# Thresholded attention and a rational feed-forward on one core: each batch by halves of its queries, and the first batch's probabilities transposed by float32 products

## The chip, the cores and the metric

One core of one Trainium2 chip runs the whole program. The metric is the device time of one execution in microseconds (us); lower is better. Three runs of the kernel before took 1432.35, 1436.73 and 1437.20 us, median 1436.73.

## The reference

There are 8 batches of 8 heads, 576 queries and keys, 64 numbers a head; the feed-forward goes from 512 to 2048 and back to 512 over 4608 tokens. Everything is float32.

```python
scores = q @ k.T / 8                                  # per batch and head
thresh = scores.max(-1) - tau                         # tau = 0.02
scores = where(scores >= thresh, scores, -1e9)
attn = exp(scores - scores.max(-1)); attn /= attn.sum(-1) + 1e-9
x = (attn @ v)                                        # heads side by side: 4608 x 512
h = x @ w_in
P = a[0] + a[1]*h + a[2]*h**2 + a[3]*h**3
Q = 1 + abs(b[0])*abs(h) + abs(b[1])*h**2
out = (P / (Q + 1e-6)) @ w_out
```

## The kernel before

**Units.** Heads go in pairs, so there are 4 pairs a batch and 32 in all (`bp`, 0 to 31). A pair's 576 queries are five units `t`: four of 128 queries (`NT` = 4) and one of the last 64, in which both heads share the 128 rows. `units` (line 504) lists them pair after pair, all five of a pair together. `pos` (lines 505 to 510) gives each its place on a scale on which a full unit counts 1 and a short one 0.5; a batch is 18 long.

**One unit** (`unit_ops`, line 611). TensorE makes the scores in float32 from QQ and KK (`f_qk`, lines 657 and 668). VectorE takes the row maxima (`f_max`: line 679 for both heads at once, line 681 for one, which the first `SINGLE` units use). ScalarE applies the threshold as a very steep Prelu (`f_pre`, line 694) and the exponential with its row sums (`f_sum`, line 698), both into a buffer `e`. The reciprocal of the sum (lines 703 to 709) scales the probabilities, which are split into a float16 high half (`f_hi`, in the buffer `hi`, written by the helper `times`, lines 280 and 282) and a low half (`f_lo`, line 720, over `e`). Both halves are transposed by DMA from the SP queue (`f_tp`, line 730) into `pT`, which holds two units. When two units are there, TensorE multiplies them with V (`f_av`, line 745): five key blocks, three float16 products for each (high by high, low by high, high by low) and each head, the two heads in different halves of the output rows. The result is split into a high and a low half of x (`f_xh`, `f_xl`, lines 753 to 759).

**V.** `load_v_ops` (line 551) loads the V tile of a pair into one of five buffers in turn (`bp % NV`), each load after the attention product that last read the buffer. When the four tiles of a batch are there, their largest absolute value gives a scale (`scale_ops`), and each tile is split into float16 halves (`split_v_ops`, lines 589 and 592).

**Q and K.** `load_ops` (line 528) loads QQ and KK of a pair once, five DMAs, from the SP queue for the first 8 pairs (`EARLY_BP`) and from POOL's queue after that; there are two buffers of each.

**Weights.** w_in and w_out come as 16 pieces of 512 KB each from POOL's queue into tiles of the pool `t`, and are decoded to float32 by ScalarE and VectorE (`decode_ops`, line 401); w_in is then scaled and split into float16 halves (lines 477 to 489). They form four blocks of 4 + 4 pieces, one for each 512 of the hidden width. `WHEN` (line 32) says for each block at which place its first piece is due and by how much the next ones follow.

**Feed-forward.** x is gathered in chunks of 256 tokens: two for the full units of each batch, ("m", batch, half), with units 0 and 1 in half 0 and units 2 and 3 in half 1, and one for the short units of four batches, ("r", ...). `moe_ops` (line 822) is one step: four slices of 128 of the hidden width for one chunk, with 48 float16 products (line 852), the rational function on ScalarE and VectorE (lines 861 to 906) and 8 float32 products with w_out (line 913, two records each). A chunk takes four steps, so there are 18 chunks and 72 steps. `last_g1` ties the steps' first products into one fixed order (`todo`): batch 0's chunks in the order of `FIRST`, then every chunk of batch b in the course of batch b + 1, and the last batch's three in the order of `LAST` behind the attention. A chunk that is interrupted leaves a partial sum, which `f_o` (line 915) evicts.

**The order.** Nothing is written out by hand. Each operation (`op`) has one engine or a choice (`FLEX`, with an estimated duration on each), a key (its due place), what it waits for, and the buffers and PSUM banks that it takes and gives back (`Hold`; `POOLS` has the number of each). `Plan.order` (line 131) simulates the engines with these durations and delays and at each moment emits the operation that can start first, the one with the lower key where several can. Buffers of a pool are handed out in the order of `rank`. Where TensorE would stand idle in the first 400 us of the plan it puts in warming products that multiply an identity (`f_warm`, line 1041). On the chip every engine runs its own list in that order and waits on semaphores. Plain DMAs and the transposes of the SP queue go out in order, as do those of POOL's queue ("GD" in the plan).

Of the kernel before, what the change touches and what calls it, by code (L numbers as in the profile page):

```python
# [23 lines left out]
POOLS = {"e": 4, "hi": 3, "pT": 2, "st": 8, "sc": 2, "t": 11, "u": 3, "x": 4, "xr": 1}  # L24
# [16 lines left out]

EARLY_BP = 8

STEEP = 2.0 ** 100

UP = 2.0 ** -14
TPD = 1.3

AHEAD_RANK = 2.0
# [7 lines left out]
        "vl": {"DVE": 0.75}, "xh": {"ACT": 0.31, "DVE": 0.31}, "xhr": {"ACT": 0.18, "DVE": 0.12}, "A": {"ACT": 0.541, "DVE": 0.345}, "r": {"ACT": 0.74, "DVE": 0.345},  # L57
# [30 lines left out]
class Plan:  # L88
# [42 lines left out]
    def order(self):  # L131
# [20 lines left out]
        while left:  # L152
# [78 lines left out]
def masked_attention_rational_ffn(  # L231
# [28 lines left out]
    for name, n in [*POOLS.items(), ("q", NQ), ("k", NQ)]:  # L260
        plan.pool(name, n)
# [242 lines left out]
    units = [(bp, t) for bp in range(NBP) for t in range(NT + 1)]  # L504
# [8 lines left out]
    NV = 5  # L513
# [5 lines left out]
    sx = const.tile([P, B], F32, name="sx")  # L519
    for t in Vs:  # L520
        nc.gpsimd.memset(t[:, NT * P:], 0.0)
    kq = {}
    av_done = {}
# [4 lines left out]
    def load_ops(bp):  # L528
        bb, pr = divmod(bp, NP)
        p = pos[(bp, 0)]  # L530
        plan.rank = p - 3.0
        kh, qh = kq[bp] = Hold("k", 2 * NT + 1), Hold("q", 2 * NT + 1)
        first = bp == 0
        p0 = p - (4.6 if first else 4.0)
        queue, eng = (nc.sync, "DMA") if bp < EARLY_BP else (nc.gpsimd, "GD")

        def ldq():
            QQ = QQs[qh.slot]
            queue.dma_start(QQ[0:D, 0:S], qT[bb, pr, :, 0:S])
# [9 lines left out]
        k_done[bp] = [op(eng, 1.1, p0 + 0.1, ldk, (), [kh])]  # L549

    def load_v_ops(bp):
        bb, pr = divmod(bp, NP)
        plan.rank = pos[(bb * NP, 0)]
        t = Vs[bp % NV]
        queue, eng = (nc.sync, "DMA") if bp < EARLY_BP else (nc.gpsimd, "GD")

        def ld():
            queue.dma_start(
                t[:, 0:NT * P].rearrange("p (c d) -> p c d", c=NT),
                v[bb, 0:NT * P, pr * P:(pr + 1) * P].rearrange("(c p) d -> p c d", p=P))  # L560
# [5 lines left out]
        def mx():  # L566
            if bb not in vms:
# [6 lines left out]
        q = pos[(bp, 0)] - 17.0  # L574
        l = op(eng, 1.6, max(q, -2.0 + 0.1 * pr), ld, [av_done.get(bp - NV)])
        hv = [Hold("u", 1)]
        vm_ops.setdefault(bb, []).append(op(FLEX["vmax"], 0, max(q + 1.0, p - 1.0), mx, [l], hv, hv))
        if pr == NP - 1:
            isx_done[bb] = scale_ops(p, lambda: vms[bb], 14, isx[:, bb:bb + 1], sx[:, bb:bb + 1], vm_ops[bb], f"x{bb}")
            for i in range(NP):  # L580
                split_v_ops(bb * NP + i)

    def split_v_ops(bp):
        bb, pr = divmod(bp, NP)
        p = max(pos[(bp, 0)] - 2.0, pos[(bb * NP, 0)])
        t, th = Vs[bp % NV], VHs[bp % NV]

        def vh():
            times(th, t, sx[:, bb:bb + 1])

        def vl():
            nc.vector.scalar_tensor_tensor(t.bitcast(F16)[:, 0:VW], t, sx[:, bb:bb + 1], th, ALU.mult, ALU.subtract)
        o = op(FLEX["vh"], 0, p, vh, [isx_done[bb]])
        v_done[bp] = op(FLEX["vl"], 0, p + 0.1, vl, [o])
# [16 lines left out]
    def unit_ops(bp, t):  # L611
# [3 lines left out]
        single = bp * (NT + 1) + t < SINGLE  # L615
        heads = (0, 1) if full else (0,)
        kh, qh = kq[bp]
        VL, VH = Vs[bp % NV].bitcast(F16)[:, 0:VW], VHs[bp % NV]
# [3 lines left out]
        e_hold = Hold("e", 1)  # L622
# [108 lines left out]

        def f_av():
            pT = place(two["pT"])
            box["av"] = bank(bhs["av"])[:, 0:w2]
# [15 lines left out]
        def f_xh():  # L750
            x = x_tile(ck)[0][:, pr, xo:xo + w2]
            if plan.eng == "ACT":
# [4 lines left out]
        def f_xl():  # L757
            xh, xl = x_tile(ck)
            nc.vector.scalar_tensor_tensor(xl[:, pr, xo:xo + w2], box["av"], UP, xh[:, pr, xo:xo + w2],
# [31 lines left out]
        his, los = [], []  # L791
        for hh in heads:
            his.append(op(FLEX["hi"], 0, p + 0.5 + 0.02 * hh, lambda hh=hh: f_hi(hh), [rec] + his, [hi_hold] if hh == 0 else ()))
            los.append(op("DVE", 0.68, p + 0.55 + 0.02 * hh, lambda hh=hh: f_lo(hh), his + los, (), [st_hold]))
        if not full:
            his.append(op("DVE", 0.13, p + 0.55, lambda: f_twice("hi"), his))
            los.append(op("DVE", 0.13, p + 0.6, lambda: f_twice("lo"), los))
        tp = op("DMA", TPD if full else 0.6 * TPD, p + 0.6, lambda: f_tp("hi"), his + two["tp"], [two["pT"]] if t % 2 == 0 else (),
                [hi_hold])
        tp = op("DMA", TPD if full else 0.6 * TPD, p + 0.65, lambda: f_tp("lo"), los + [tp], (), [e_hold])  # L800
        two["tp"].append(tp)
# [3 lines left out]
        av = op("PE", 2.0 if full else 0.7, p + 1.2, f_av, two["tp"] + [v_done[bp]], [bh], [two["pT"]])  # L805
        av_done[bp] = av
# [5 lines left out]
        xh = op(FLEX["xh" if full else "xhr"], 0, p + 1.4, f_xh, [av] + ([x_done[ck][0]] if not first else []), first, [bh])  # L812
# [9 lines left out]
    def moe_ops(ck, f0, nb, p, begins, ends, soon):  # L822
# [4 lines left out]
        plan.rank = p = max(p, w_key(g, 2 * NC))  # L827
# [87 lines left out]
        def f_o(tt, old):  # L915
# [3 lines left out]
            else:  # L919
                o = place(obox[tt]["hold"])  # L920
                nc.scalar.activation(o, acc[tt], AF.Copy, scale=-1.0)
# [53 lines left out]
        if ends:  # L975
            prev = None
            obox = {}
            for tt in range(2):
                old = sums.get((ck, tt))
                obox[tt] = {}  # L980
                if old is None:
                    ho = obox[tt]["hold"] = Hold("u", 1)
                    o = op("ACT", 0.5, p + 0.2 * nb + 1.8, lambda tt=tt, old=old: f_o(tt, old), [last_g2[tt], prev], [ho], [ah[tt]])
# [4 lines left out]
                if f0 + nb == NF:  # L988
# [5 lines left out]
    load_ops(0)  # L994
    for i in range(NP):
        load_v_ops(i)
    for bp, t in units:
        unit_ops(bp, t)
        if t == NT and bp + 1 < NBP:
            load_ops(bp + 1)  # L1000
        if t == NT and bp + NP < NBP:
            load_v_ops(bp + NP)
    todo = []
    for bb in range(B):
# [5 lines left out]
        last = pos[(bb * NP + NP - 1, NT)]  # L1010
# [4 lines left out]
        steps = []  # L1015
        if bb % 4 == 0 and bb:
            steps += [(("r", bb // 4 - 1, 0), f) for f in range(0, NF, NC)]
        if bb:
            steps += [(("m", bb - 1, c), f) for c in range(2) for f in range(0, NF, NC)]
        p0 = pos[(bb * NP, 0)] + LEAD  # L1020
        step = NP * 4.5 / len(steps) if steps else 0
        if bb == 1:

            steps = [(("m", 0, c), f) for c, f0, f1 in FIRST for f in range(f0, f1, NC)]
            step -= LEAD0 / len(steps)
            p0 += LEAD0
        todo += [(ck, f, NC, p0 + i * step) for i, (ck, f) in enumerate(steps)]
# [56 lines left out]
```

## Time and profile before

| | |
|---|---|
| median of three runs | 1436.73 us |
| the profiled execution, its own time | 1437.0 us |
| its span, first to last instruction | 1435.2 us |
| TensorE (PE) busy | 1365.4 us, 95%, 9130 instructions |
| VectorE (DVE) busy | 1194.6 us, 83% |
| ScalarE (ACT) busy | 1164.4 us, 81% |
| GpSimd (POOL) busy | 165.4 us, 12% |
| mean granted TensorE clock | 0.976 |
| read from and written to HBM | 45.09 MB and 9.44 MB |
| transposes issued | 320, each 3.3 us from issue to landing in the median |

The page gives busy time of each engine, also in 40 equal slices (a digit is tenths of the slice), the granted clock, and the share of the 16 DMA engines in use. "PEld" are weight loads, which run beside products. Busy time by stretch can be asked for any span of time and for one line alone. The waits name the engine and line that waited, what ended the wait, and total, times and longest. A line such as 280, 282 or 287 is that of a helper and serves several operations.

### The profile page before, as it was taken

How to read it: one execution, taken by the hardware profiler on the slowest of the kernel's cores; microseconds unless marked ns; L12 is line 12 of the kernel's file. 1: busy time of each engine (PE TensorE's matmuls, PEld its weight loads, DVE VectorE, ACT ScalarE, POOL GpSimd, SP SyncE). 2: the span in 40 equal slices, each digit the busy share in tenths (PEclk: the TensorE clock that was granted, in tenths of full speed). 3: DMA queues.
4: the chain of work that ended last, by engine and by line, in shares of the span. 5: the costliest groups of instructions: out<-in, count | busy, mean ns of one | idle time of the engine just before them, and what ended most of it. 6: DMA issues, size and time to landing. Idle time of an engine off the chain costs nothing. (4 is left out here: it accounts for less than half of the span.)

```text
span 1435.2 us, 24320 instructions
## 1 busy us (share of the span) xinstructions
PE 1365.4 (95%) x9130; PEld 859.8 (60%) x9130; DVE 1194.6 (83%) x1782; ACT 1164.4 (81%) x2078; POOL 165.4 (12%) x310
## 2 busy tenths in 40 slices
PE   8489889999999999999999999999999999999998
PEld 6366666566565566646666656665665656575664
DVE  5488798989987979788888987898987988896665
ACT  6489999999898988889768777889888978874553
POOL 3100111111111010111010111102011100000000
PEclk8698999999999999999999999999999999999999
DMA  8986775555565454545343354536555464420000
GB/s 238 141 167 125 154 165 120 121 101 121 105 115 101 82 114 91 100 101 115 73 89 80 74 90 92 114 65 131 90 97 112 82 108 93 90 43 16 15 16 15
DMA packets 371749, 142.12 MB, mean 99 GB/s; under 512 B 353328, under 2 KB 358576, under 8 KB 371632
## 3 DMA queue, kind: packets, MB, share of 16 engines
q1 hardware_dynamic: 355248, 93.11, 37.6%
q0 software_dynamic: 16384, 47.46, 12.5%
q8 instruction: 72, 1.18, 0.3%
q14 instruction: 45, 0.37, 0.1%
HBM read 45.09 MB, written 9.44 MB: 38 GB/s over the span
## 5 line engine op out<-in xcount | busy, mean ns | idle before, releaser
L913 PE MATMUL banks<-wp,t 128*128 128x512 f32 x1152 | 527.2, 598 | 4.3 <-DVE t L906 3.3
L852 PEld LDWEIGHTS <-wi 128*128 128x128 f16 x3456 | 336.6, 99 | 88.7 <-issue 52.1
L852 PE MATMUL banks<-x,wi 128*128 128x256 f16 x3072 | 362.5, 273 | 3.9 <-ACT t L861 1.7
L913 PEld LDWEIGHTS banks<-wp,t 128*128 128x128 f32 x1152 | 206.5, 190 | 209.8 <-issue 200.9
L720 DVE SCALAR_TENSOR_TENSOR e<-e,st,hi 128x576 f16<-128x576 f32 x288 | 234.1, 813 | 14.8 <-ACT hi L280 10.8
L694 ACT ACTIVATE e<-banks,st,cf 128x576 f32<-128x576 f32 x288 | 231.5, 825 | 17.7 <-DVE st L688 12.7
L657 PE MATMUL banks<-KK,QQ 64*128 64x512 f32 (+3 forms) x784 | 224.4, 552 | 22.0 <-ACT e L694 18.2
L698 ACT ACTIVATE e<-e,cf 128x576 f32<-128x576 f32 x288 | 220.7, 772 | 0.4
L280 ACT ACTIVATE hi<-e,st 128x576 f16<-128x576 f32 x254 | 190.6, 769 | 24.3 <-DVE st L709 20.0
L745 PE MATMUL banks<-pT,VH 128*64 128x256 f16 (+1 forms) x1920 | 136.3, 254 | 29.6 <-DMA pT<-e 28.7
L861 ACT ACTIVATE t<-banks,hsc 128x512 f32<-128x512 f32 (+1 forms) x192 | 106.1, 574 | 71.0 <-PE banks L852 70.5
L657 PEld LDWEIGHTS banks<-KK,QQ 64*128 64x128 f32 (+1 forms) x784 | 91.3, 194 | 117.9 <-issue 50.5
L679 DVE TENSOR_REDUCE st<-banks 128x2 f32<-128x1152 f32 x108 | 145.7, 1349 | 16.4 <-PE banks L668 16.1
L745 PEld LDWEIGHTS <-VH 128*64 128x64 f16 x1920 | 87.0, 112 | 62.1 <-issue 48.2
L891 ACT ACTIVATE t<-t,cf 128x1024 f32<-128x1024 f32 (+1 forms) x73 | 82.8, 1134 | 39.7 <-DVE t L888 39.4
L745 PE MATMUL banks<-pT,V 128*64 128x256 f16 (+1 forms) x960 | 109.4, 252 | 0.0
L668 PEld LDWEIGHTS banks<-KK,QQ 128*128 128x128 f32 x432 | 56.3, 190 | 81.9 <-issue 81.9
L900 DVE SCALAR_TENSOR_TENSOR t<-t,t 128x1024 f32<-128x1024 f32 (+1 forms) x73 | 88.0, 1205 | 15.3 <-ACT t L894 14.8
L906 DVE SCALAR_TENSOR_TENSOR t<-t,cf,t 128x1024 f32<-128x1024 f32 (+1 forms) x73 | 92.5, 1267 | 0.8
L897 DVE SCALAR_TENSOR_TENSOR t<-t,cf,t 128x1024 f32<-128x1024 f32 (+1 forms) x73 | 92.3, 1265 | 0.2
L888 DVE TENSOR_TENSOR t<-t,t 128x1024 f32<-128x1024 f32 (+1 forms) x73 | 87.9, 1205 | 2.8 <-ACT t L873 2.6
L903 DVE SCALAR_TENSOR_TENSOR t<-t,t 128x1024 f32<-128x1024 f32 (+1 forms) x73 | 88.0, 1206 | 0.8
(93 smaller groups left out, 1422.6 us busy)
## 6 DMA issues: line engine op xcount, KB each, us to landing
t<-in_w_in_dram POOLq DMA_DIRECT2D x16, 512.0 KB, 5.7
t<-in_w_out_dram POOLq DMA_DIRECT2D x16, 512.0 KB, 5.7
out_dram<-u POOLq DMA_DIRECT2D x32, 256.0 KB, 2.7
KK<-in_kT_dram POOLq DMA_DIRECT2D x48, 144.0 KB, 4.3
V<-in_v_dram POOLq DMA_DIRECT2D x24, 256.0 KB, 4.1
QQ<-in_qT_dram POOLq DMA_DIRECT2D x24, 144.0 KB, 3.0
QQ<-in_qT_dram POOLq DMA_DIRECT2D x24, 128.0 KB, 3.6
pT<-hi SPq DMA_TRANSPOSE x160, 3.3
```

The source lines that it names most:

```text
L280: nc.scalar.activation(dst, src, AF.Identity, scale=factor)
L657: nc.tensor.matmul(dst, QQ[r, c0:c0 + P], KK[r, k0:k1], **kw)
L679: nc.vector.tensor_reduce(box["st"][:, 0:2], box["both"], AX.X, ALU.max, negate=True)
L694: nc.scalar.activation(ev(hh), box["s"][hh], AF.Prelu, scale=qscale, bias=box["st"][:, 2 + hh:3 + hh], alpha=STEEP)
L698: nc.scalar.activation(e, e, AF.Exp, bias=ntau, accum_out=box["st"][:, 4 + hh:5 + hh])
L720: nc.vector.scalar_tensor_tensor(box["lo"][:, c], ev(hh), box["st"][:, 6 + hh:7 + hh], box["hi"][:, c], ALU.mult, ALU.subtract)
L745: nc.tensor.matmul(dst, V[:, c * P + hh * D:c * P + (hh + 1) * D], rhs, start=c == 0 and n == 0, stop=c == NT and n == 2)
L852: nc.tensor.matmul(d, wi_tile(c, f0 + j, hl), x[:, c, :], start=c == 0 and n == 0, stop=c == NC - 1 and n == 2)
L861: nc.scalar.activation(box["h3"][:, 2 * k:2 * k + 2, sl], psv[:, :, sl], AF.Identity, scale=hsc[:, b2, g:g + 1])
L897: nc.vector.scalar_tensor_tensor(box["r"], box["r"], a1, box["h"], ALU.add, ALU.mult)
L906: nc.vector.scalar_tensor_tensor(box["r"], box["r"], a0, box["q"], ALU.add, ALU.mult)
L913: nc.tensor.matmul(acc[tt], box["r"][:, o:o + P], wo[f], start=begins and j == 0, stop=ends and j == nb - 1)
```

## The change

**Order.** A batch is now visited in seven visits: pairs 0, 1 and 2 with units 0 and 1 only, pair 3 with all five units, then pairs 2, 1 and 0 with units 2, 3 and 4. `load_ops` runs once a visit, so q and k of three pairs of each batch are loaded twice. The V buffers become a pool of five that each V tile takes and gives back after the last of its three attention products. `VISITED` = 8 makes all batches go this way.

**Transposes.** In the first batch (`is_plain`: pairs 0 to 3, units 0 to 3) the probabilities are not split and not transposed by DMA. VectorE writes the identity times the reciprocal sum of each row (`f_diag`), TensorE multiplies each 128 by 128 block of e with it (`f_tr`, ten float32 products in three banks), and three evictions bring the result to `pT` in float32 (`f_ev`). The attention product then is ten float32 products with the V tile as loaded (`f_avp`), and x is scaled by another factor. The first batch's short units go as before, and V is split when these need it.

**Feed-forward.** Chunk ("m", 0, 0) starts with its first two steps, then follow the four of ("m", 0, 1), then the other two. From there every step's key is at least `SPACING` = 1.9679 behind the one before (3.0642 in batch 0) and `LEAD` = 0.8676 behind the last unit of its chunk. The partial sums of the interrupted chunk share one tile of the pool `t`.

**Weights, pools, constants.** The weights' due places move from (-3.82, 14.74, 15.84, 25.03) to (-3.45, 5.0, 11.9, 15.21). `e` has 3 buffers for 4, `hi` 2 for 3, `u` 4 for 3, `xr` 2 for 1. The plan counts a DMA of the SP queue that starts before 120 us at twice its duration and 1 us more. Priorities between ScalarE and VectorE change.

```diff
-POOLS = {"e": 4, "hi": 3, "pT": 2, "st": 8, "sc": 2, "t": 11, "u": 3, "x": 4, "xr": 1}
+POOLS = {"e": 3, "hi": 2, "pT": 2, "st": 8, "sc": 2, "t": 11, "u": 4, "x": 4, "xr": 2}
...
-LEAD, LEAD0 = 2.88, 0.04
-ENDK, ENDS = 1.2, 1.3
+LEAD, SPACE0, SPACING = 0.8676, 3.0642, 1.9679
+ENDK, ENDS = 3.4139, 5.1328
-WHEN = [(-3.82, 1.63), (14.74, 0.95), (15.84, 1.27), (25.03, 1.06)]
-SINGLE = 25
-FIRST = [(0, 0, 12), (1, 0, 16), (0, 12, 16)]
+WHEN = [(-3.45, 1.43), (5.0, 0.76), (11.9, 0.29), (15.21, 0.9)]
+V0, V1 = -2.1791, 0.6179
+SINGLE = 22
+VISITED = 8
+FIRST = [(0, 0, 8), (1, 0, 16), (0, 8, 16)]
+NV = 5
+PLAIN = (0, 1, 2, 3)
-AHEAD_RANK = 2.0
+AHEAD_RANK = 2.54
...
-EARLY = {"ACT": 2.4, "DVE": 6}
-EARLY_END = 250
-PRICE = {"ACT": 1.0, "DVE": 2.0}
+EARLY = {"ACT": 2.3035, "DVE": 3.83}
+EARLY_END = 543.1302
+PRICE = {"ACT": 0.6687, "DVE": 1.9849}
+LOADS_END = 120.0
...
+            if e == "DMA" and t < LOADS_END:
+                o.dur = 2.0 * o.dur + 1.0
...
-    units = [(bp, t) for bp in range(NBP) for t in range(NT + 1)]
+    half, rest = list(range(NT // 2)), [NT]
+    other = list(range(NT // 2, NT))
+    visits = []
+    for bb in range(B):
+        v0 = bb * NP
+        if bb < VISITED:
+            visits += [(v0 + i, half) for i in range(NP - 1)] + [(v0 + NP - 1, half + other + rest)]
+            visits += [(v0 + i, other + rest) for i in range(NP - 2, -1, -1)]
+        else:
+            visits += [(v0 + i, half + other + rest) for i in range(NP)]
+    units = [(bp, t) for bp, ts in visits for t in ts]
...
-        e_hold = Hold("e", 1)
+        e_hold = Hold("e", (3 if full else 2) if is_plain(bp, t) else 1)
...
+        def f_diag(hh):
+            if hh == 0:
+                box["dg"] = place(dg_hold)
+            nc.vector.tensor_scalar(box["dg"][:, hh * P:(hh + 1) * P], ident, box["st"][:, 6 + hh:7 + hh], None, ALU.mult)
+        def f_tr(piece, hold):
+            e, d = box["e"], bank(hold)
+            if piece < 2:
+                for c in range(NT):
+                    k = piece * (S + REM) + c * P
+                    nc.tensor.matmul(d[:, c * P:(c + 1) * P], e[:, k:k + P], box["dg"][:, piece * P:(piece + 1) * P],
+                                     start=True, stop=True)
+            else:
...
+        def f_ev(piece, hold):
+            pT = flat(two)
+            c0, n = ((0, NT), (NT + 1, NT), (NT, 1))[piece]
+            copy(pT[:, c0:c0 + n, t % 2, :], bank(hold)[:, 0:n * P].rearrange("p (c k) -> p c k", c=n))
...
+        def f_avp():
+            pT, V = flat(two), Vs[vh_[bp].slot]
+            box["av"] = bank(bhs["av"])[:, 0:w2]
+            for c in range(NT + 1):
+                for hh in range(2):
...
+                    nc.tensor.matmul(dst, V[:, c * P + hh * D:c * P + (hh + 1) * D], rhs, start=c == 0, stop=c == NT)
...
+        if plain:
+            pieces = (0, 1, 2) if full else (0, 2)
+            dg_hold = Hold("u", len(pieces))
...
+            for piece in pieces:
+                hold = Hold("b", 1, B1)
+                tr = op("PE", 0.9 if piece < 2 else 0.3, p + 0.5, lambda x=piece, h=hold: f_tr(x, h), [dg], [hold],
+                        [e_hold, dg_hold])
...
-    load_ops(0)
-    for i in range(NP):
-        load_v_ops(i)
-    for bp, t in units:
-        unit_ops(bp, t)
-        if t == NT and bp + 1 < NBP:
-            load_ops(bp + 1)
-        if t == NT and bp + NP < NBP:
-            load_v_ops(bp + NP)
+    for bp in range(NBP):
+        load_v_ops(bp)
+    for bp, ts in visits:
+        load_ops(bp, ts)
+        for t in ts:
+            unit_ops(bp, t)
...
+    order = [(("m", 0, c), range(f0, f1, NC)) for c, f0, f1 in FIRST]
+    for bb in range(1, B - 1):
+        order += [(("m", bb, c), range(0, NF, NC)) for c in range(2)]
+        if bb % 4 == 3:
+            order.append((("r", bb // 4, 0), range(0, NF, NC)))
+    p = 0.0
+    for ck, fs in order:
...
+        ready = max(pos[x] for x in last) + LEAD
+        for f in fs:
+            p = max(p + (SPACE0 if bb == 0 else SPACING), ready)
+            todo.append((ck, f, NC, p))
```

More of the change, by code (lines that the diff above doesn't have):

```diff
@@ L259, in masked_attention_rational_ffn @@
     op = plan.op
-    for name, n in [*POOLS.items(), ("q", NQ), ("k", NQ)]:
+    for name, n in [*POOLS.items(), ("q", NQ), ("k", NQ), ("v", NV)]:
         plan.pool(name, n)
@@ L519, in masked_attention_rational_ffn @@
     sx = const.tile([P, B], F32, name="sx")
+    sxu = const.tile([P, 1], F32, name="sxu")
     for t in Vs:
         nc.gpsimd.memset(t[:, NT * P:], 0.0)
-    kq = {}
-    av_done = {}
+    kq, vh_, v_loaded, plain_av = {}, {}, {}, {}
     k_done, q_done, v_done, isx_done = {}, {}, {}, {}
@@ L526, in masked_attention_rational_ffn, with load_ops @@
     pairs = {}
-    def load_ops(bp):
+    def load_ops(bp, ts):
         bb, pr = divmod(bp, NP)
-        p = pos[(bp, 0)]
+        p = pos[(bp, ts[0])]
         plan.rank = p - 3.0
-        kh, qh = kq[bp] = Hold("k", 2 * NT + 1), Hold("q", 2 * NT + 1)
-        first = bp == 0
+        n = sum(2 if t < NT else 1 for t in ts)
+        kh, qh = kq[bp] = Hold("k", n), Hold("q", n)
+        first = p == 0
         p0 = p - (4.6 if first else 4.0)
@@ L549, in load_ops, with is_plain, v_low @@
         k_done[bp] = [op(eng, 1.1, p0 + 0.1, ldk, (), [kh])]
+    def is_plain(bp, t):
+        return bp < NP and t in PLAIN
+    v_ops = {}
+    def v_low(bp):
+        if bp not in v_done:
+            p, o, vl = v_ops[bp]
+            v_done[bp] = op(FLEX["vl"], 0, p + 0.1, vl, [o] + plain_av.get(bp, []))
+        return v_done[bp]
     def load_v_ops(bp):
@@ L614, in unit_ops @@
         full = t < NT
-        single = bp * (NT + 1) + t < SINGLE
+        single = units.index((bp, t)) < SINGLE
         heads = (0, 1) if full else (0,)
         kh, qh = kq[bp]
-        VL, VH = Vs[bp % NV].bitcast(F16)[:, 0:VW], VHs[bp % NV]
+        plain = is_plain(bp, t)
         nh = len(heads)
@@ L730, in f_tp, with flat @@
             nc.sync.dma_start_transpose(place(two["pT"])[:, t % 2, part == "lo", 0:nb, :], box[part][:, 0:nb * P])
+        def f_diag(hh):
[11 more added lines that the diff above has]
+                for hh in range(2):
+                    k, dg = (NT * P + hh * REM, hh) if full else (NT * P, 0)
+                    nc.tensor.matmul(d[hh * D:(hh + 1) * D, 0:P], e[:, k:k + REM], box["dg"][:, dg * P:(dg + 1) * P],
+                                     start=True, stop=True)
+        def f_ev(piece, hold):
+            pT = flat(two)
+            c0, n = ((0, NT), (NT + 1, NT), (NT, 1))[piece]
+            copy(pT[:, c0:c0 + n, t % 2, :], bank(hold)[:, 0:n * P].rearrange("p (c k) -> p c k", c=n))
+        def flat(two):
+            return place(two["pT"]).rearrange("p a b c d -> p (a b c d)").bitcast(F32).rearrange(
+                "p (c u k) -> p c u k", c=2 * NT + 1, u=2)
+        def f_avp():
+            pT, V = flat(two), Vs[vh_[bp].slot]
+            box["av"] = bank(bhs["av"])[:, 0:w2]
+            for c in range(NT + 1):
+                for hh in range(2):
+                    pp = slice(hh * D, (hh + 1) * D)
+                    dst = box["av"][pp, :]
+                    if full:
+                        rhs = pT[:, c if hh == 0 or c == NT else NT + 1 + c, :, :]
+                        dst = dst.rearrange("p (u k) -> p u k", u=2)
+                    else:
+                        rhs = pT[:, c, 0, hh * REM:(hh + 1) * REM]
+                    nc.tensor.matmul(dst, V[:, c * P + hh * D:c * P + (hh + 1) * D], rhs, start=c == 0, stop=c == NT)
         def f_av():
             pT = place(two["pT"])
+            VL, VH = Vs[vh_[bp].slot].bitcast(F16)[:, 0:VW], VHs[vh_[bp].slot]
             box["av"] = bank(bhs["av"])[:, 0:w2]
@@ L751, in f_xh @@
             x = x_tile(ck)[0][:, pr, xo:xo + w2]
-            if plan.eng == "ACT":
+            if plain:
+                times(x, box["av"], sxu)
+            elif plan.eng == "ACT":
                 nc.scalar.activation(x, box["av"], AF.Copy, scale=UP)
@@ L790, in unit_ops @@
         rec = op("DVE", 0.103, p + 0.4, f_rec2, [rec])
[L791 to L801, printed above, removed]
+        if plain:
+            pieces = (0, 1, 2) if full else (0, 2)
+            dg_hold = Hold("u", len(pieces))
+            dg = None
+            for hh in heads:
+                dg = op("DVE", 0.14, p + 0.45, lambda hh=hh: f_diag(hh), [rec, dg], [dg_hold] if hh == 0 else (), [st_hold])
+            for piece in pieces:
+                hold = Hold("b", 1, B1)
+                tr = op("PE", 0.9 if piece < 2 else 0.3, p + 0.5, lambda x=piece, h=hold: f_tr(x, h), [dg], [hold],
+                        [e_hold, dg_hold])
+                take = [two["pT"]] if not two["tp"] and t % 2 == 0 else ()
+                two["tp"].append(op(FLEX["ev" if piece < 2 else "ev1"], 0, p + 0.55, lambda x=piece, h=hold: f_ev(x, h),
+                                    [tr] + two["tp"][:1], take, [hold]))
+        else:
+            his, los = [], []
+            for hh in heads:
+                his.append(op(FLEX["hi"], 0, p + 0.5 + 0.02 * hh, lambda hh=hh: f_hi(hh), [rec] + his, [hi_hold] if hh == 0 else ()))
+                los.append(op("DVE", 0.68, p + 0.55 + 0.02 * hh, lambda hh=hh: f_lo(hh), his + los, (), [st_hold]))
+            if not full:
+                his.append(op("DVE", 0.13, p + 0.55, lambda: f_twice("hi"), his))
+                los.append(op("DVE", 0.13, p + 0.6, lambda: f_twice("lo"), los))
+            tp = op("DMA", TPD if full else 0.6 * TPD, p + 0.6, lambda: f_tp("hi"), his + two["tp"], [two["pT"]] if t % 2 == 0 else (),
+                    [hi_hold])
+            tp = op("DMA", TPD if full else 0.6 * TPD, p + 0.65, lambda: f_tp("lo"), los + [tp], (), [e_hold])
+            two["tp"].append(tp)
@@ L804, in unit_ops @@
         bh = bhs["av"] = Hold("b", 2, B1)
-        av = op("PE", 2.0 if full else 0.7, p + 1.2, f_av, two["tp"] + [v_done[bp]], [bh], [two["pT"]])
-        av_done[bp] = av
+        if plain:
+            av = op("PE", 2.6 if full else 0.7, p + 1.2, f_avp, two["tp"] + [v_loaded[bp]], [bh], [two["pT"], vh_[bp]])
+            plain_av.setdefault(bp, []).append(av)
+        else:
+            av = op("PE", 2.0 if full else 0.7, p + 1.2, f_av, two["tp"] + [v_low(bp)], [bh], [two["pT"], vh_[bp]])
         if ck not in xh_hold:
@@ L811, in unit_ops @@
             first = []
-        xh = op(FLEX["xh" if full else "xhr"], 0, p + 1.4, f_xh, [av] + ([x_done[ck][0]] if not first else []), first, [bh])
+        xh = op(FLEX["xh" if full else "xhr"], 0, p + 1.4, f_xh, [av, isx_done["up"]] + ([x_done[ck][0]] if not first else []), first, [bh])
         xl = op("DVE", 0.36 if full else 0.16, p + 1.5, f_xl, [xh], (), [bh])
@@ L826, in moe_ops @@
         g = f0 // NC
[L827 removed]
+        plan.rank = p = max(p, w_key(g, 2 * NC) - 1.0)
         name = f"{kind}{bb}_{half}_{f0}"
@@ L977, in moe_ops @@
             obox = {}
+            through = f0 + nb == NF
+            part = Hold("t", 2)
             for tt in range(2):
@@ L981, in moe_ops @@
                 if old is None:
-                    ho = obox[tt]["hold"] = Hold("u", 1)
-                    o = op("ACT", 0.5, p + 0.2 * nb + 1.8, lambda tt=tt, old=old: f_o(tt, old), [last_g2[tt], prev], [ho], [ah[tt]])
+                    ho = obox[tt]["hold"] = Hold("u", 1) if through else part
+                    o = op("ACT", 0.5, p + 0.2 * nb + 1.8, lambda tt=tt, old=old: f_o(tt, old), [last_g2[tt], prev], [ho] if through or tt == 0 else [], [ah[tt]])
                 else:
@@ L1014, in masked_attention_rational_ffn @@
             hsc_done[bb] = [op("DVE", 0.13, last, f_hscs, [isx_done[bb]] + sw_done)] * NW
[L1015 to L1027, printed above, removed]
+    order = [(("m", 0, c), range(f0, f1, NC)) for c, f0, f1 in FIRST]
[5 more added lines that the diff above has]
+    for ck, fs in order:
+        kind, bb, c = ck
+        last = [(bp, t) for bp in range(NBP) for t in range(NT + 1) if x_chunk(bp // NP, t)[0] == ck]
+        ready = max(pos[x] for x in last) + LEAD
+        for f in fs:
+            p = max(p + (SPACE0 if bb == 0 else SPACING), ready)
+            todo.append((ck, f, NC, p))
     steps = [(ck, f) for ck in [(("m", B - 1, 0), ("m", B - 1, 1), ("r", B // 4 - 1, 0))[i] for i in LAST] for f in range(0, NF, NC)]
```

35 lines of the change are left out of this document (22 added, 13 removed).

## The prediction, made before the changed kernel had run

> **What bounds the kernel now.** I read the page's slices first, then busy time by stretch, then the waits and transfers of the one bad stretch, then how far each kind of work had come by 200 us.
>
> ```profile
> span 1435.2 us, 24320 instructions
> PE   8489889999999999999999999999999999999998
> DVE  5488798989987979788888987898987988896665
> ACT  6489999999898988889768777889888978874553
> PEclk8698999999999999999999999999999999999999
> DMA  8986775555565454545343354536555464420000
> ```
>
> One slice is 35.9 us. From the sixth slice on TensorE is full and its clock whole; before that nothing is full all the time, and the second slice has a hole on every compute engine while the DMA row stands at 9. In stretches (columns: length, busy and instructions of PE, weight loads, DVE, ACT, POOL, granted clock, DMA share, GB/s):
>
> ```profile
> 0.00:20.00 20.00, 15.07 (x55) 11.71 (x56) 7.44 (x21) 9.16 (x17) 5.05 (x24) 0.75 0.73 207
> 20.00:47.00 27.00, 22.72 (x124) 17.39 (x122) 23.59 (x53) 25.55 (x55) 9.80 (x21) 0.88 1.07 259
> 47.00:66.00 19.00, 0.92 (x8) 0.48 (x8) 2.69 (x8) 1.57 (x4) 1.06 (x3) 0.50 1.15 122
> 66.00:200.00 134.00, 113.86 (x893) 85.63 (x890) 113.36 (x245) 121.67 (x254) 11.66 (x23) 0.89 0.75 151
> 200.00:1284.00 1084.00, 1068.12 (x7342) 657.62 (x7344) 950.16 (x1367) 934.31 (x1651) 132.39 (x230) 1.00 0.51 98
> 1284.00:1435.00 151.00, 144.69 (x728) 86.94 (x720) 97.39 (x92) 72.14 (x101) 5.40 (x10) 0.99 0.05 15
> ```
>
> After 200 us TensorE is busy for all but 16 of 1084 us, and in the tail for all but 6 of 151: only less product work, or work done sooner, helps there. The front is another matter. From 47 to 66 us everything stands, and the waits and the transfers of that place name the cause: the second half of an attention product waits for a transposed tile, which is late because the DMA engines carry the weights as well.
>
> ```profile
> PE banks L745 <- DMA pT<-e: 18.1, 1, 18.1
> DMA to landing us min/median/max: 2.5/3.3/22.5
> ```
>
> Part of what TensorE does in the front is no work at all but the warming products of line 1041:
>
> ```profile
> 0.00:200.00 200.00, 56.31 (x349) 50.59 (x350) 0.84 0.83 169
> 200.00:1284.00 1084.00, 7.05 (x54) 6.42 (x54) 1.00 0.51 98
> ```
>
> And the feed-forward's first products (line 852, 48 to a step of four slices of the hidden width) come only after 160 us:
>
> ```profile
> 0.00:160.00 160.00, 0.00 (x0) 0.00 (x0) 0.81 0.83 171
> 160.00:180.00 20.00, 7.26 (x48) 5.08 (x48) 0.91 0.58 111
> 0.00:200.00 200.00, 12.66 (x96) 9.78 (x96) 0.84 0.83 169
> ```
>
> So the front is limited by VectorE and ScalarE, which must do attention and decode the weights before there is anything else for TensorE, and by 19 us of DMA. A "unit" below is 128 queries of a pair of heads, a step as above.
>
> **The price of a unit, a weight piece and a step.** Progress is counted by the exponentials of line 698 (two records a head, so four a unit; each row below has 2 per head), the decoding of line 430 (one a piece, 32 in all) and line 906 (one a step):
>
> ```profile
> 0.00:200.00 200.00, 37.47 (x90) 0.84 0.83 169
> 200.00:1284.00 1084.00, 199.07 (x486) 1.00 0.51 98
> 0.00:200.00 200.00, 14.98 (x22) 0.84 0.83 169
> 200.00:1284.00 1084.00, 75.57 (x59) 1.00 0.51 98
> ```
>
> That is 45 heads or 22.5 units and 22 pieces by 200 us, and 121.5 units, 10 pieces and 59 steps from 200 to 1284. The tail holds about 12 steps, so a step takes (97.39 + 72.14)/12 = 14.1 us of VectorE and ScalarE together. Two equations for a unit u and a piece d: 121.5u + 10d = 950.16 + 934.31 - 59 x 14.1 = 1052.6, and 22.5u + 22d = 305 (the first four stretches summed) less 14 for the two steps half begun = 291. They give d = 4.8 and u = 8.3 us. On TensorE a step is read off the chain of waits of the steady part, as is an attention product of two tiles:
>
> ```profile
> 1208.03 5.24 PE banks L852 x48
> 1274.81 6.87 PE banks L913 x16
> 1186.35 1.76 PE banks L745 x30
> ```
>
> A step is 5.24 + 6.87 = 12.1 us, and a unit (1068.12 - 7.05 - 59 x 12.1)/121.5 = 2.86 us. By 200 us TensorE has done 22.5 x 2.86 + 2 x 5.24 = 75 us of work, so the front costs 125 us of the run, and the 7 us of warming after it make 132. This is all the change can attack.
>
> **The change, part by part.**
>
> *Transposes by products (16 units of the first batch).* Gone per unit are two high halves, two low halves and two DMA transposes; new are two scaled diagonals, ten float32 products and three evictions. The nearest rows (the diagonal by line 360, the eviction by line 861, which also reads 512 float32 from PSUM):
>
> ```profile
> L280 ACT ACTIVATE hi<-e,st 128x576 f16<-128x576 f32 x254 | 190.6, 769 | 24.3 <-DVE st L709 20.0 <-issue 2.2 <-DVE st L705 0.7
> L720 DVE SCALAR_TENSOR_TENSOR e<-e,st,hi 128x576 f16<-128x576 f32 x288 | 234.1, 813 | 14.8 <-ACT hi L280 10.8
> L360 DVE TENSOR_SCALAR u<-ident,sc 128x128 f32<-128x128 f32 x12 | 3.4, 282 | 0.1
> L861 ACT ACTIVATE t<-banks,hsc 128x512 f32<-128x512 f32 x128 | 86.6, 679 | 49.7 <-PE banks L852 49.3
> ```
>
> Removed: 2 x 0.77 + 2 x 0.81 = 3.16 us. Added: 2 x 0.28 + 2 x 0.68 + 0.3 for the short eviction (an estimate: under half the long one) = 2.2 us. A unit falls from 8.3 to 7.3 us. On TensorE a warming product has the shape of a transposing one; at full clock:
>
> ```profile
> 180.00:200.00 20.00, 4.62 (x34) 4.05 (x34) 1.00 1.02 208
> ```
>
> 4.62/34 = 0.136 us a record, two records a product: 0.27 us, and 16 units x 10 products = 43 us at most. A float32 product of 512 columns takes 6.87/8 = 0.86 us, a float16 one of 256 takes 5.24/48 = 0.11: four times as much a column. The attention product has a third as many, so 1.76 x 4/3 = 2.3 us if the two heads still overlap, twice that if not: 4 to 23 us over the 8 tile pairs, and I take 5, since the float16 ones overlap. Together 48 us more TensorE work, all of it in the front. Its cover is the idle and warming time there; without that cover it is the slow rival below.
>
> *DMA.* The first batch then transposes only its four short units, so the 18.1 us wait should go; next late is a weight piece or the decode itself. The transfers from 40 to 70 us (queue: packets, MB, share of 16 engines):
>
> ```profile
> q1 hardware_dynamic: 4550, 1.39, 55.2%
> q0 software_dynamic: 720, 2.62, 46.6%
> ```
>
> The queue with the transposes took 40% a MB, that of the weights 18%, so what leaves is the dear half. The Trainium skill (Advanced Engine Details and Errata, X-Bar Transpose (TRN2)) says instead that transposing DMAs are as fast as ordinary ones; by that rule what leaves is worth only its bytes, the engines stay full of weights and the wait moves to those. These two rows disagree by 2.2 times, though the first queue carries q and k too.
>
> *Order and weights.* Half of the queries of all heads are done by unit 8 instead of unit 18, so the first two steps can run there, on weights due at unit 8 and 11. The products of the third need the other half, at unit 17.4 by the new keys, and then one step falls due per 3.06 units. To that point the front must do 16 x 7.3 + 2 x 8.3 = 133 us of attention, 28 pieces (four of the last block are due later) x 4.8 = 134, and 2 x 14.1 = 28: 296 us of VectorE and ScalarE. The start, 0 to 20 us, gives 16.6. What rate then? From 66 to 200 us the two made (113.36 + 121.67)/134 = 1.75 us per us, from 20 to 47 us 1.82, and at best, from 180 to 200:
>
> ```profile
> 180.00:200.00 20.00, 16.45 (x158) 13.39 (x157) 19.27 (x36) 19.16 (x33) 3.57 (x7) 1.00 1.02 208
> ```
>
> 1.92. I take 1.82, the stretch ahead of the stall, since the DMA waits inside the 1.75 mostly go. Then the point is reached at 20 + 279/1.82 = 173 us, with 18 x 2.86 + 2 x 12.1 = 76 us of lasting product work done: a loss of 97. TensorE's load to there is 76 + 48 = 124 us, or 139 at the clock of 0.89 that 66 to 200 us shows, under 173. After it a step with 3.06 units wants (14.1 + 25.4)/1.82 = 21.7 us against 20.9 on TensorE: 0.8 us lost six times, 5 us. Loss 102 against 132.
>
> *Reloads.* Three of four pairs per batch load q and k twice: 24 visits more, 18 on POOL's queue, where V loads and result stores stand behind them and TensorE's scores wait. Their cost is nothing while these loads wait for their buffer and not for the queue, which now is so:
>
> ```profile
> POOL QQ L539 <- PE banks L657: 309.4, 20, 33.0
> POOL V L558 <- PE banks L745: 349.6, 24, 23.7
> ```
>
> The last V tile of the next batch finds its buffer free at unit 15.5 of 18 instead of 13.5: two units of 1084/121.5 = 8.9 us less slack, of about 6.5. Nothing, unless that chain takes over 4 units.
>
> *Smaller rings.* e has three buffers for four, hi two for three. One e is held from line 694 to the landing of its second transpose:
>
> ```profile
> 635.08 0.83 ACT L694 ACTIVATE e<-banks,st,cf 128x576 f32<-128x576 f32 x1
> 641.62 1.33 SPq L730 DMA_TRANSPOSE pT<-e  x1
> ```
>
> That is 6.5 + 3.3 = 9.8 us, 1.1 buffers at 8.9 us a unit; nothing. The partial sums' move and three fewer single-head units cost nothing either: same instructions, the former hidden beside full TensorE.
>
> **The sum.** 1437.0 (this execution; its span is 1435.2, the median of the runs 1436.7) - 132 + 102 = **1407 us**. At 1.75 us per us the point is at 179.5 us and the steps lose 10: 1418. At 1.92 it is at 165 us with no loss after: 1394.
>
> **Rivals.** *The products are not hidden* (slower). If scores, transposes, evictions and attention products follow each other on TensorE instead of overlapping ScalarE, its 48 us lengthen the front: 1407 + 48 = 1455 us. It decides once TensorE's work to unit 18, waits included, passes 173 us, and cancels the gain at 203. For it: the front's clock averaged 0.84, and each piece needs a bank and an eviction before the next. Against: 139 of 173 us.
> *The stall stays under another name.* The weights are due up to ten units sooner, so 18 us of waiting return: 1425 us. For it: the DMA share was already 1.07 ahead of the hole. The rule of equal speed in the Trainium skill (Advanced Engine Details and Errata, X-Bar Transpose (TRN2)) leads here; the two queues' rows above speak against it.
> *A denser front*: 1.92, 1394 us.
> *It does not do what it says*: attention still uses up VectorE and ScalarE first, the two early steps merely displace units, and nothing moves: 1437.
>
> **Chances.** Forecast 0.50, denser 0.13, stall kept 0.12, nothing 0.11, not hidden 0.14. Half a per cent, 7 us, is about what a measurement here can tell from no change. Faster by more: 0.50 + 0.13 + 0.12, less 0.02 for a stall of 25 us = 0.73; within: 0.11 + 0.02 = 0.13; slower: 0.14. The range 1388 to 1438 takes in all but the slow rival and the best third of the dense one.
>
> **What would show it.** Right: no wait of over 5 us for a transposed tile before 100 us; first products of line 852's kind before 100 us and the third step's near 173; VectorE plus ScalarE over 300 us by 173; warming of line 1041 well under 56 us; the steady part again idle under 2%. Wrong: TensorE over 95% busy at full clock before 150 us, waits for weights of over 10 us, or scores waiting for QQ or e in each visit.

## The result and the profile after

The changed kernel takes **1397.34 us** in the median of four runs, the kernel before 1436.97 us beside it: a ratio of 0.971, 95% interval 0.9643 to 0.9778. One of the four, 1430.25 us, ran at a granted clock of 0.94 where the other three had 0.99, and the ratio leaves it out. The forecast was 1407 us. The profiled execution took 1398.17 us with a span of 1396.4.

The page of the changed kernel (one slice is 34.9 us):

```profile
span 1396.4 us, 24502 instructions
PE 1361.7 (98%) x9138; PEld 854.4 (61%) x9138; DVE 1179.8 (84%) x1791; ACT 1164.4 (83%) x2082; POOL 209.5 (15%) x400
PE   8998999999999999999999999999999999999996
DVE  5988999699898988789887989888888988787664
ACT  6987989898988888888898998889888989884652
PEclk8999999999999999999999999999999999999998
DMA  9335344756655644566456565746556555340000
```

The hole in the second slice is gone on every engine, the DMA row falls from 9 to 3 there, and the granted clock is nine tenths or more from the second slice on. Busy TensorE hardly moved, 1365.4 to 1361.7 us, although it has new products to do: 34.7 us of warming went, and the products that make the scores (`f_qk`) took 224.7 us instead of 236.8, with a mean clock in the first 200 us of 0.96 instead of 0.84. The share of the DMA engines adds up the time that packets took, and so can pass 1. By stretch (length, busy and instructions of PE, weight loads, DVE, ACT, POOL, clock, DMA share, GB/s):

```profile
0.00:20.00 20.00, 16.05 (x86) 13.64 (x87) 10.93 (x29) 9.65 (x20) 6.35 (x26) 0.91 0.86 229
20.00:47.00 27.00, 25.06 (x164) 20.53 (x163) 19.97 (x57) 22.25 (x45) 8.62 (x20) 0.87 0.90 254
47.00:66.00 19.00, 18.35 (x116) 12.52 (x114) 18.65 (x51) 18.06 (x42) 0.18 (x1) 1.00 0.23 76
66.00:200.00 134.00, 126.81 (x904) 86.03 (x903) 122.34 (x273) 115.72 (x234) 18.20 (x34) 0.97 0.43 113
200.00:1284.00 1084.00, 1075.01 (x7382) 660.62 (x7380) 940.56 (x1321) 945.91 (x1667) 171.80 (x311) 1.00 0.55 108
1284.00:1396.00 112.00, 100.42 (x498) 61.08 (x496) 67.33 (x66) 52.77 (x78) 4.31 (x8) 0.97 0.05 15
```

From 47 to 66 us, where TensorE did 0.92 us of work, it now does 18.35, all but 0.94 of it real work, with the DMA share at 0.23 instead of 1.15. The new products by group (two records a product; line 789 the eight large blocks of a unit, 794 the two small ones, 819 the attention product, 782 the diagonal, 285 most of the evictions):

```profile
L789 PE MATMUL banks<-u,e 128*128 128x128 f32 x256 | 33.1, 281 | 1.8 <-DVE u L782 1.5 <-DVE pT L287 0.3
L794 PE MATMUL banks<-u,e 128*64 128x128 f32 x64 | 7.0, 298 | 0.0
L819 PE MATMUL banks<-pT,V 128*64 128x256 f32 x160 | 21.2, 416 | 3.2 <-ACT pT L285 3.2
L782 DVE TENSOR_SCALAR u<-ident,st 128x128 f32<-128x128 f32 x32 | 8.8, 282 | 0.1
L285 ACT COPY pT<-banks 128x512 f32<-128x512 f32 x32 | 18.4, 583 | 3.4 <-PE banks L789 3.2
```

The attention products they replace took 8 x 1.76 = 14.1 us, so TensorE has 33.1 + 7.0 + 21.2 - 14.1 = 47.2 us more to do; the prediction said 48. Against that stands the warming, in the first 300 us, first the kernel before and then the changed one:

```profile
0.00:300.00 300.00, 63.37 (x402) 57.01 (x402) 0.89 0.74 151
```

```profile
0.00:300.00 300.00, 28.67 (x170) 26.41 (x170) 0.97 0.54 135
```

Progress to the predicted point, 173 us, in the changed kernel (feed-forward first products, exponentials, decoded pieces, then all engines):

```profile
0.00:173.00 173.00, 13.03 (x114) 10.93 (x115) 0.95 0.53 147
0.00:173.00 173.00, 32.06 (x76) 0.95 0.53 147
0.00:173.00 173.00, 20.29 (x30) 0.95 0.53 147
0.00:173.00 173.00, 160.58 (x1054) 114.66 (x1055) 145.03 (x360) 143.22 (x304) 28.21 (x74) 0.95 0.53 147
```

76 records are 38 heads or 19 units, 30 pieces are decoded, two steps are done and the third has begun (114 of 144 first products).

### The profile page after: what moved, and what is told of

It reads as the page before. It is cut to its first block, busy times and chain, and to the rows that moved or that the text cites. A ratio compares the mean times of both kernels' runs of the same rounds, so it can differ in the third digit from the quotient of the medians.

```text
span 1396.4 us, 24502 instructions
## 1 busy us (share of the span) xinstructions
PE 1361.7 (98%) x9138; PEld 854.4 (61%) x9138; DVE 1179.8 (84%) x1791; ACT 1164.4 (83%) x2082; POOL 209.5 (15%) x400
## 3 DMA queue, kind: packets, MB, share of 16 engines
q1 hardware_dynamic: 319760, 87.21, 34.7%
## 5 line engine op out<-in xcount | busy, mean ns | idle before, releaser
L766 DVE SCALAR_TENSOR_TENSOR e<-e,st,hi 128x576 f16<-128x576 f32 x256 | 208.0, 813 | 21.8 <-ACT hi L293 18.5
L703 PE MATMUL banks<-KK,QQ 64*128 64x512 f32 (+3 forms) x776 | 214.1, 540 | 8.5 <-ACT e L740 7.3
L293 ACT ACTIVATE hi<-e,st 128x576 f16<-128x576 f32 x208 | 157.2, 768 | 31.4 <-DVE st L755 21.4
L703 PEld LDWEIGHTS banks<-KK,QQ 64*128 64x128 f32 (+1 forms) x776 | 86.7, 187 | 102.8 <-issue 46.0
L835 PE MATMUL banks<-pT,VH 128*64 128x256 f16 (+1 forms) x1760 | 117.2, 247 | 2.7 <-DMA pT<-e 2.6
L1009 DVE SCALAR_TENSOR_TENSOR t<-t,t 128x1024 f32<-128x1024 f32 (+1 forms) x73 | 87.9, 1204 | 16.5 <-ACT t L1003 16.0
L835 PE MATMUL banks<-pT,V 128*64 128x256 f16 (+1 forms) x880 | 95.7, 245 | 0.0
L835 PEld LDWEIGHTS <-VH 128*64 128x64 f16 x1760 | 75.4, 110 | 29.8 <-issue 25.1
L564 POOL DMA_DIRECT2D QQ<-in_qT_dram x42 | 22.0, 524 | 476.2 <-PE banks L703 271.0
```

Source lines behind the costliest of these rows:

```text
L293: nc.scalar.activation(dst, src, AF.Identity, scale=factor)
L703: nc.tensor.matmul(dst, QQ[r, c0:c0 + P], KK[r, k0:k1], **kw)
L766: nc.vector.scalar_tensor_tensor(box["lo"][:, c], ev(hh), box["st"][:, 6 + hh:7 + hh], box["hi"][:, c], ALU.mult, ALU.subtract)
L835: nc.tensor.matmul(dst, V[:, c * P + hh * D:c * P + (hh + 1) * D], rhs, start=c == 0 and n == 0, stop=c == NT and n == 2)
```

## The experiments

Each ratio is to the kernel before, measured beside it, with its 95% interval; times are medians. The changed kernel stands at 0.971.

**Taking the parts away.** Without the products, without the order, and without both:

```diff
-PLAIN = (0, 1, 2, 3)
+PLAIN = ()
```

> The changed kernel with every probability tile of the first batch split and transposed by DMA again (PLAIN empty), all else as changed. Theory A (the prediction's: the front is limited by VectorE, ScalarE and the DMA engines, the float32 products are hidden there): 16 units cost 1 us more of VectorE and ScalarE each, 9 us at 1.82 us per us, and 64 transposes go beside the weights again: 1406 to 1424 us, with waits for a transposed tile of over 5 us before 100 us. Rival (the products are on the path): up to 47 us faster than the changed kernel, 1350 to 1390 us.

```diff
-VISITED = 8
+VISITED = 0
```

> The changed kernel with the old order of visits, every pair with all five units (VISITED 0), products and timing kept. Theory A: no step can run before unit 18; the point where steps follow each other comes 28/1.82 = 15 us sooner, but with 24 us less product work done: 9 us slower, about 1406 us. Rival (the order is nearly the whole gain): over 1425 us. Rival (the order brings nothing): 1395 to 1400 us.

With both edits:

> The changed kernel with both parts undone (PLAIN empty, VISITED 0): what is left is the new timing of the weights, the first steps, the plan's slower DMA, rings and constants. Theory A: both losses together, 1415 to 1433 us. Rival (earlier weights and the plan's constants are the gain): 1402 us or less.

| | products | no products |
|---|---|---|
| halves | 0.971 (0.9643 to 0.9778), 1397.3 us | 1.0217 (1.0164 to 1.0269), 1466.9 us |
| pair by pair | 0.9911 (0.988 to 0.9943), 1421.4 us | 1.0124 (1.0054 to 1.0195), 1449.6 us |

(The expectation's 64 transposes are 32: two a unit.) All three came out slower than theory A said: both parts were priced too low. The products are worth 5% with the order and 2% without it; the order is worth 2% with the products and nothing without them (0.9% the wrong way, with intervals that overlap). Alone, the new dates, rings and constants lose 1.2%. So the products gain with the order and without it, and the order gains only with the products. The rival that the products are on the path is out, by its sign. In the kernel without the products the front's first 200 us hold 79 us of warming, where the changed kernel has 28, and transposes land late again, up to 18.9 us after issue. But the waits that the expectation named did not come: TensorE waits for a transposed tile for 4.0 us in all in these 200 us. So here the loss shows as warming, which the plan puts in, and not as a stall:

```profile
0.00:200.00 200.00, 79.06 (x566) 74.38 (x566) 0.88 0.78 164
```

**The same products where TensorE is full.** `is_plain` and the factor `sxu` are extended to the fourth batch as well:

```diff
+BATCHES = (0, 3)
...
-        return bp < NP and t in PLAIN
+        return bp // NP in BATCHES and t in PLAIN
```

> The changed kernel with the fourth batch's 16 full units transposed by float32 products too, in the stretch where TensorE is full. Theory A (the products cost nothing only because the front has room for them): 40 us of transposing and 7 us of longer attention products land on the path, 1437 to 1444 us. Rival (TensorE's busy time has slack everywhere, or VectorE's relief is worth as much): 1395 to 1410 us.

1437.4 us, ratio 1.0023 (0.9997 to 1.005), 40 us above the changed kernel. By the same rows as above, the fourth batch's products add 31.8 + 7.0 + 16.9 us and replace 14.1, which is 41.6 us, so nearly all of it lands on the path. Its page has TensorE at 1399.0 us busy, 37 more. The products pay in the front because it has idle and warming time to give.

**Is it the plan or the DMA engines?** The kernel without products is planned with every early transpose at twice its time and 1 us more. Three runs try the plan's part by itself:

```diff
-LOADS_END = 120.0
+LOADS_END = 0.0
```

> The changed kernel without the plan's doubling of early DMA times (LOADS_END 0), products and order kept. Only the short units of the first batch and what comes after it before 120 us are transposed by DMA, so both theories expect little: 1393 to 1405 us. If the doubling is worth much by itself, because it brings q, k and V loads forward: over 1410 us.

With `PLAIN = ()` besides:

> The changed kernel with all transposes by DMA (PLAIN empty) and the plan's doubling of early DMA times taken out (LOADS_END 0). The run without the products alone came out 70 us slower, far beyond the 9 to 27 us expected; its plan counts each early transpose at 3.6 us in a row. Theory P (the plan is what spoils that kernel: it keeps TensorE waiting and warming): most of it comes back, 1410 to 1435 us. Theory D (the DMA engines themselves hold the front up, whatever the plan says): 1455 to 1480 us.

And the doubling put into the kernel before:

> The kernel before with one thing of the change, the plan's doubling of DMA times of the SP queue before 120 us. Theory A (the 18 us stall is the chip's, the DMA engines are full; a plan that knows it can only arrange work around it): 1420 to 1437 us, the stall spread over several shorter waits. Theory P (such a plan delays attention in the front): over 1445 us.

The changed kernel without the doubling: 1409.95 us, 0.981 (0.9779 to 0.9842), outside the 1393 to 1405 us expected and just short of the 1410 at which the doubling would be worth much by itself. Without products and doubling: 1452.2 us, 1.0107 (1.006 to 1.0155), between the theories and nearer to the DMA engines. The kernel before with the doubling: 1465.4 us, 1.0189 (1.0159 to 1.022), on the plan's side: it warms for 89 us where it had warmed for 63. So the doubling costs 1 to 2% where there are many early transposes and seems to gain 1% where there are few (0.971 against 0.981, intervals that just meet). With the plan's part away, products are still worth 1.0107 against 0.981, 3%. What is left of the transposes' harm shows in the waits of the first 200 us of the kernel without products and doubling, and in its stretch from 47 to 66 us:

```profile
ACT e L740 <- DMA pT<-e: 17.6, 5, 11.1
```

```profile
47.00:66.00 19.00, 10.47 (x46) 8.93 (x45) 8.76 (x16) 10.03 (x21) 2.45 (x7) 0.62 1.15 238
```

ScalarE waits for a buffer `e` whose transpose has not landed, for 17.6 us, and the hole at 47 us is back in part, with the DMA share at 1.15: TensorE is busy for 10.47 of 19 us, and 6.88 of that is warming. The transfers from 40 to 70 us of the two kernels without the doubling, first with products and no transpose in this stretch, then without products and with five transposes (queue: packets, MB, share of 16 engines):

```profile
q0 software_dynamic: 859, 3.12, 31.7%
q1 hardware_dynamic: 400, 0.59, 6.9%
```

```profile
q1 hardware_dynamic: 7245, 2.55, 55.5%
q0 software_dynamic: 1004, 3.65, 45.3%
```

The loads of q and k are the same in both, so the transposes add 1.96 MB and 48.6% to the hardware queue, 25% a MB, beside 12% a MB for the software queue with the weights (10% without the transposes).

**How far does the order count?** Only the first batch by halves, then the first two (`VISITED` = 2):

```diff
-VISITED = 8
+VISITED = 1
```

> The changed kernel with only the first batch visited by halves (VISITED 1), the other seven pair by pair as before. Theory A (the order matters only in the front, where steps for TensorE are wanting): 1393 to 1402 us, with 21 visits' loads of q and k fewer. Rival (halves are worth something in every batch, a finished half being ready for the feed-forward sooner): 1408 to 1425 us.

> The changed kernel with the first two batches visited by halves, the other six pair by pair. With the first alone it was 55 us slower than the changed kernel: at 300 us the feed-forward had done exactly batch 0's 8 steps and waited for batch 1. Theory S (a feed-forward that has caught up runs dry at each batch that is finished whole, so every batch by halves counts): still 1425 to 1450 us, with TensorE idle over 20 us between 300 and 1284 us. Theory E (only that first handover counts): 1395 to 1405 us.

1452.6 us, 1.0098 (1.0068 to 1.0128), and 1435.8 us, 0.9963 (0.9933 to 0.9993). The first lies above both ranges expected for it, the second in that of theory S. The theories by which only the front, or only the first handover, counts are wrong. First products of the feed-forward by 300 us, the changed kernel first, then the one with the first batch alone by halves:

```profile
0.00:300.00 300.00, 59.13 (x512) 49.77 (x513) 0.97 0.54 135
```

```profile
0.00:300.00 300.00, 44.41 (x384) 37.32 (x384) 0.99 0.53 130
```

384 is eight steps of 48, all of batch 0 and nothing of batch 1, whose halves come only with its last pair. The feed-forward has caught up with attention and runs dry. The kernel with two batches by halves has 522 there, no fewer than the changed one, but 1422 by 700 us where the changed one has 1548. From 300 to 1284 us, in the changed kernel, with one batch by halves, and with two:

```profile
300.00:1284.00 984.00, 975.38 (x6693) 597.95 (x6691) 851.49 (x1197) 852.16 (x1501) 163.20 (x296) 1.00 0.54 106
```

```profile
300.00:1284.00 984.00, 952.29 (x6435) 581.85 (x6434) 818.34 (x1139) 825.51 (x1472) 112.26 (x201) 0.98 0.49 94
```

```profile
300.00:1284.00 984.00, 949.31 (x6472) 578.58 (x6470) 825.45 (x1161) 834.51 (x1485) 114.48 (x204) 0.98 0.50 95
```

TensorE is idle for 9, 32 and 35 us, and in the last two the clock is lower too. So these two kernels lose what they had behind the front. That a caught-up feed-forward runs dry can't be the whole cause, though: the kernel with no batch by halves has exactly 384 products at 300 us too, with all weights decoded and as many heads done (139 records of the exponential against 138), yet it is idle for only 15 us from 300 to 1284 and ends 31 us before the one with one batch by halves. Why one batch by halves does worse than none stays open; how much the step spacing of 1.97 units has to do with it was not tried apart. The kernel before, which spaces 2.25 and starts later, is idle for 14 us there.

**The rings.** The kernel before with three buffers `e` and two `hi`:

```diff
-POOLS = {"e": 4, "hi": 3, "pT": 2, "st": 8, "sc": 2, "t": 11, "u": 3, "x": 4, "xr": 1}
+POOLS = {"e": 3, "hi": 2, "pT": 2, "st": 8, "sc": 2, "t": 11, "u": 3, "x": 4, "xr": 1}
```

> The kernel before with the rings of the change, e three buffers for four and hi two for three. The prediction put their cost at nothing, since one e is held 9.8 us and a unit takes 8.9: within 0.5% of the kernel before. Rival (in the front a transpose lands up to 22.5 us late, so a fourth buffer was in use there): 10 to 25 us slower.

1460.8 us, 1.0147 (1.0096 to 1.0198): the rival was right. The cost sits in the front. From 300 to 1284 us TensorE is idle for 12 us, against 14 before, but in the first 200 us ScalarE waits for `e` for 13.7 us, where it had waited 3.1. Which of the two rings costs how much was not parted.

```profile
ACT e L694 <- DMA pT<-e: 13.7, 4, 10.3
```

**The queues.** All loads of q, k and V on the SP queue:

```diff
-EARLY_BP = 8
+EARLY_BP = 32
```

> The changed kernel with all loads of q, k and V on the SP queue beside the transposes (EARLY_BP 32), so that POOL's queue holds weights and results only. Prediction's claim (the reloads cost nothing on POOL's queue, the loads wait for their buffers): 1394 to 1402 us, unless the SP queue's transposes now wait behind a load for its buffer, which would make it 1405 us or more. Asked besides: POOL's last drain took 10.3 us in the changed kernel and 4.4 in the one before; if its length goes with the number of DMAs that POOL issued, it is 2 to 4 us here.

1405.3 us, 0.976 (0.9711 to 0.9809): by the medians inside the miss that the expectation named, though the interval meets the changed kernel's. TensorE's idle time from 300 to 1284 us doubles to 17 us, and the SP queue waits 101.5 us for buffers of q where it had waited 43.7, with transposes behind. That the reloads cost nothing on POOL's queue is thus not contradicted; with the other loads on the SP queue they seem to cost.

**More products.** The first batch's short units too, and no splitting of its V:

```diff
-PLAIN = (0, 1, 2, 3)
+PLAIN = (0, 1, 2, 3, 4)
```

> The changed kernel with the first batch's four short units transposed by products too, so that its V needs no splitting either. Theory A (the front is limited by VectorE, ScalarE and DMA): 4 V tiles' splits of 1.7 us and the short units' halves and copies go, some 10 us of VectorE and ScalarE or 5 us of time, and 8 DMA transposes: 1388 to 1396 us. Rival (the front is now limited by TensorE): 4 times about 2.3 us of products more, 1399 to 1407 us.

1395.6 us, 0.9693 (0.9638 to 0.9748): the median lies at the edge of theory A's range and below the rival's, but it cannot be told from the changed kernel, so neither theory is confirmed.

## Why the prediction held, and where it did not

- **The front's limit.** Predicted: 296 us of VectorE and ScalarE to the point at 173 us. Measured to 173 us: 145.03 + 143.22 = 288 us, with a unit and two pieces more than asked. So the forecast's own sign of over 300 us by 173 did not come. The price of a piece, 4.8 us, was too high: its operations in the kernel before (lines 422, 426, 430, 470 and 486 and their helpers) add up to 4.1 us of VectorE and ScalarE a piece. And the rate of 1.82 was too good: from 20 to 47 us it was 42.2/27 = 1.56, and from 66 us on 238/134 = 1.78. From 20 to 173 us it comes to (288 - 21)/153 = 1.75, the rate that the forecast had set aside, which would have given 1418 us. The two errors cancel, so that the point came out near 173 us is in part luck. What held the two engines back from 20 to 47 us stays open: neither waits for a weight there, and the longest sum of waits is 4.9 us of VectorE for an exponential.
- **Lasting work.** 19 x 2.86 + 2 x 12.1 + 18 x 0.11 = 80.5 us by 173 us, a loss of 92 us where 97 were forecast. From there to 300 us TensorE is idle for 1.7 us and warms for 1.4, where 5 us were allowed.
- **The steady part** gained what the sum left out: idle from 200 to 1284 us fell from 16 to 9 us. The step that failed is that the order is worth two steps in the front and nothing behind it. The run without halves lost 24 us against 9. In the front the 9 us are borne out: to 300 us TensorE is idle or warming for 52.0 us there and for 42.8 in the changed kernel. Behind 300 us the run without halves is idle for 15 us instead of 9, and its clock is 0.99 instead of 1.00. That a finished half keeps the feed-forward supplied at each batch fits this, but the visits' runs don't prove it.
- **The products' price on TensorE** was right to a microsecond, as a sum: the transposes took 40.1 us instead of 43, the attention products 7.1 more instead of 5. That the front hides it is shown by the run without the products and the one with the fourth batch's. Their worth was mis-sized: 1 us a unit of vector work and an 18 us wait were counted, 3% (some 42 us) remain with the plan's part taken out.
- **"Smaller rings: nothing"** was wrong as reasoned. It took the hold of a steady unit, 9.8 us, for all; in the front a landing took up to 22.5 us. In the changed kernel's first batch products, and not the DMA, free `e` for the full units; that it escapes the cost for this reason is argued from the waits, since no run had products and four buffers.
- **The stall kept under another name** did not come: no wait for a DMA transpose stands among those of the first 173 us, the first one is issued at 100.7 us, and the DMA share was 0.23 where it had been 1.15, weights sooner or not. The Trainium skill's rule that transposing DMAs are as fast as ordinary ones (Advanced Engine Details and Errata, X-Bar Transpose (TRN2)) is not borne out in this mix by the engines' time: 25% a MB against 12%, in the rows from 40 to 70 us above. In landing time the trace of the kernel before agrees with it: over the whole run a transpose lands after 3.3 us in the median, and a 256 KB load of V on POOL's queue after 4.1; but from 40 to 70 us its three transposes took 16.8 to 22.5. What followed from the rule, that the engines stay full of weights and the wait moves to those, did not come: the longest wait of VectorE or ScalarE for a weight to 173 us is 6.4 us, at the start.
- **The end** costs more than before: TensorE's last product ends 44 us sooner, the span only 39. POOL's closing drain, as the profile calls this entry of its queue, takes 10.3 us against 4.4.

In sum: 1407 forecast, 5 us less loss to the point, 2 less behind it, 7 less in the steady part, 5 more at the end: 1398, and 1398.2 measured. Under 2 us from 200 to 300 us are counted twice in this.

## What to carry to other kernels

Where one engine is full for nine tenths of the run, look for the stretch where it is not, and price an edit by that stretch's scarce engine: the same kind of products gained 2 to 5% at the start and cost 40 us in the middle. An early gain need not last to the end: one batch by halves was 31 us worse than none, so follow the consumer's progress through every later handover. Price a ring by its longest hold, not by the usual one.

## What was not expected of the hardware

POOL's closing drain has a length that differs from program to program: 10.3 us in every profiled kernel with 400 POOL instructions, 4.2 to 4.4 us in those with 310, yet 6.5 us with 118 (all loads on SP). The changed kernel's and the last one's:

```profile
L1191 POOLq DRAIN  x3: 45/102/10287, 1385.3 to 1396.1; - x3
```

```profile
L1191 POOLq DRAIN  x3: 40/93/6526, 1396.4 to 1403.4; - x3
```

So it does not simply grow with the number of instructions or DMAs; what sets it stays open.
